# A list-scheduling planner is given TensorE's switch costs, the wait of a dependent operation, a fixed engine for early products, and other seeds

## The chip, the core and the metric

The kernel runs on one core of a Trainium2 chip. The metric is the time of one execution on the device in microseconds. The profiled execution is one such run with the hardware profiler on; its span goes from the first to the last recorded instruction and is a little shorter than its own time.

## The reference

Attention with a decaying state (per batch, head and step), then a feed-forward block with a spatial mixing over the 768 steps. Sizes: 4 batches, 8 heads, 768 steps, 48 dimensions per head (384 in all), 1024 hidden units.

```python
for t in range(S):
    cur = np.einsum('bhd,bhe->bhde', u[None] * kt, vt)
    y[:, :, t] = np.einsum('bhd,bhde->bhe', rt, state + cur)
    state = w[None, :, :, None] * state + np.einsum('bhd,bhe->bhde', kt, vt)
...
h = np.maximum(x @ w_in, 0.0)
u, v = (h[..., :d_ff // 2], h[..., d_ff // 2:])
v_n = (v - mu) / np.sqrt(var + 1e-06)
v_s = np.einsum('ts,bsd->btd', w_spatial, v_n) + b_spatial[None, :, None]
return ((u * v_s) @ w_out).astype(np.float32)
```

x is the attention's y with the heads side by side; mu and var are taken over v's 512 columns.

## The kernel before

The attention is worked in 24 chunks of 128 steps (6 for each batch). For chunk m, `load_chunk` brings the tiles rk, rs, ks and rkv; `prep` scales rk by the decays (L569 on GpSimd or L571 on VectorE for the first 13 chunks, one VectorE operation at L575 for the others), makes three products of rs and ks and one of diag with dg, reduces rs to dg (L580), and from chunk 8 on copies parts of rk into the tile A. TensorE then has three short steps for the chunk, called the mixer's: `scores` (s, 32 matmuls of 64x64, L611), `products` (r, 32 or 16 matmuls of 64x48, L630), both into one PSUM tile ps, and `apply` (y, 64 to 96 matmuls of 128x32 by 64 columns, L692) into xp. Between them `state` masks the scores (L659), carries the state from chunk to chunk (L673, L677, L679) and copies blocks for y. `fin` splits y into a high part (L332) and a low part (L729) of x.

The feed-forward tiles are made of matmuls of 128x128 by 384 or 512 columns in three terms, high by high, high by low and low by high (L735, L736, L737): `moe_v` and `moe_u` (x by w_in), `moe_sp` (spatial mixing, in a form with seven products), `moe_out` (by w_out). Between them stand the normalization of v, splits into high and low parts (`split_v`), and the gate. In the beginning VectorE, ScalarE and TensorE turn the weights, which come as 64-bit numbers, into high and low parts (`from_f64`, L457 to L480).

None of the order is written by hand. Every step is a task in `Plan`: it has one or more ways (engine and estimated cost), the tasks before it, the buffers that it takes, and a due time. `dues` works the due times out backwards from a nominal order of TensorE's tiles. `shake` then shifts the due times and the engines' leanings at random, once for each number in `SEEDS`. `run` plays the tasks through in time: it takes for each engine the best of the ready tasks, by a key that puts those that can start at once (within 0.02 us) first, by due time, and those that can start only later behind; the task's instructions are emitted in that order. A task with several ways gets the engine on which it would end first, with a `lean` added to discourage one. `BEHIND` and `SIGNAL` are the times from an operation's end to another engine's start; before the change a task on the same engine as its predecessor could start at the predecessor's end:

```python
can = max([clear] + [b.free if b.engine == e else b.end + SIGNAL[e] for b in t.before])
late = at <= free.get(e, 1.0) + 0.02
key = (0, t.due, t.place) if late else (1, at, t.due, t.place)
```

`Clock` and `Fetch` model TensorE's clock and its instruction fetch. All loads and most stores are issued by SP's queue in the planner's order (L344, L375).

Of the kernel before, what the change touches and what calls it, by code (L numbers as in the profile page):

```python
# [19 lines left out]
P = 128  # L20
# [20 lines left out]
AHEAD = 0.3  # L41
ALONE = 1000.0
CALM, LATE = 80.0, dict(DVE=1.0, SP=1.0)
SEEDS = (654236, 40537, 227094, 802348, 927760, 243010, 847265, 669742, 767280, 592966, 398425, 483486, 769239,
         558881, 534905, 557774, 619884, 911825, 37087, 256776, 431103, 948404, 736101, 744100, 112095, 746069,
         318923, 577348, 283095, 953310, 564408, 778876, 669839, 55107, 864631, 805599, 160787, 198409, 373592,)
BIAS = dict(DVE=3.0, ACT=3.5)
MOST_IN, MOST_OUT = 2, 1


BEHIND = dict(PE=0.2, DVE=0.08, ACT=0.094, POOL=0.055, SP=0.0)
SIGNAL = dict(PE=0.05, DVE=0.03, ACT=0.03, POOL=0.08, SP=0.03)
# [10 lines left out]
class Task:  # L63
    def __init__(self, ways, lag, nominal):
        self.ways, self.lag, self.nominal = [Way(*w) for w in ways], lag, nominal
        self.cost = min(w.cost for w in self.ways)
        self.engine = None
# [45 lines left out]
class Plan:  # L113
# [92 lines left out]
    def run(self):  # L206
# [4 lines left out]
        count = {k: len(u) for k, u in self.users.items()}  # L211
        last = dict.fromkeys(self.users, 0.0)
        free, line, landed, clock, fetch, bank = {}, 0.0, [], Clock(), Fetch(), {}
        self.port = 0.0
        while ready:
            best, ahead = {}, dict(free)
            for t in sorted(ready, key=lambda t: (t.due, t.place)):
                takes = [k for k in t.bufs if k not in self.slot]
                if any(len(self.slots[k[0]]) <= self.spare(k, count) for k in takes):
                    continue  # L220
                if any(k[0] in self.FIFO and self.turn[k] != self.given.get(k[0], 0) for k in takes):
                    continue
                clear = max([1.0] + [min(self.slots[k[0]])[0] for k in takes])
                found = None
                for way in t.ways:
                    e = way.engine
                    can = max([clear] + [b.free if b.engine == e else b.end + SIGNAL[e] for b in t.before])
                    if t.bank:
                        can = max([can] + [x + SIGNAL[e] for o, x in bank.items() if o != e])
                    at = max(can, ahead.get(e, 1.0)) if len(t.ways) > 1 else max(can, free.get(e, 1.0))  # L230
                    if way.nbytes:
                        at = max(self.lane(at, landed), t.due - self.AHEAD_IN)
                    end = (self.landing(line, at, way.nbytes) if way.nbytes else at + self.shared_cost(way, at)) + (way.lean if t.due < CALM or way.lean > 99.0 else LATE.get(e, 0.0))
                    if found is None or end < found[0]:
                        found = (end, e, can, way)
                _, e, can, way = found
                at = max(can, free.get(e, 1.0))
                if way.nbytes:
                    at = max(self.lane(at, landed), t.due - self.AHEAD_IN)
                if can <= ahead.get(e, 1.0) + AHEAD and not way.nbytes:  # L240
                    ahead[e] = max(can, ahead.get(e, 1.0)) + way.cost
                late = at <= free.get(e, 1.0) + 0.02
                key = (0, t.due, t.place) if late else (1, at, t.due, t.place)
                if e not in best or key < best[e][0]:
                    best[e] = (key, at, t, way)
            if not best:
# [39 lines left out]
def fused_kernel(ctx, tc, rkT, rkvE, rkvL, wT, uB, w_in, w_sp, b_sp, w_out, out):  # L286
    nc = tc.nc
    E = mybir.EngineType
    for e in (E.PE, E.DVE, E.Activation, E.Pool, E.SP):
        ctx.enter_context(tc.manual_schedule(engines={e}))  # L290
    EARLY, STATS, EC = 13, 1, FIRST_CHUNKS
    CLASSIC = (0,)
    SUM_IN, SUM_OUT = range(NK), []
    LOAD_IN = {0: -50.0, 1: -50.0}
# [15 lines left out]
    def pe(cost, f, r, w, count, nominal=None, holds=()):  # L310
        behind = 0.11 if count > 15 and count % 9 and count % 4 == 0 else 0.2
        plan.add([("PE", cost, f, False, 0, 0.0, behind)], r, w, nominal=nominal, holds=holds).count = count
# [248 lines left out]
    def prep(m):  # L561
# [12 lines left out]
        else:  # L574
            dve(1024, lambda: nc.vector.tensor_tensor(out=rk(), in0=rk(), in1=tt.unsqueeze(1).to_broadcast(  # L575
                [P, 2, NP, C]), op=ALU.mult), [RK, *TT], [r_, k_], cost=1.14, two=True)
        n_, k0 = (lambda: T[RS]), (lambda: T[KS])
        pair(DM, lambda: dict(out=n_(), in0=n_(), in1=k0(), op=ALU.mult), [RS, KS], [rn], lean=LEAN)
        pair(DM, lambda: dict(out=n_(), in0=n_(), in1=ub, op=ALU.mult), [rn, ("c", "ub")], [rn], lean=LEAN)
        dve(DM - 8, lambda: nc.vector.tensor_reduce(out=tile_of(DG, [P, H]), in_=n_().rearrange("s (h d) -> s h d", h=H),  # L580
                                                axis=AX.X, op=ALU.add), [rn], [DG])
        pair(DM, lambda: dict(out=k0(), in0=k0(), in1=tn_f, op=ALU.mult), [KS, rn, *TN], [kn], lean=LEAN)
        pair(432, lambda: dict(
            out=a().rearrange("s b q z t -> s (b q z) t"), in0=diag.unsqueeze(1).to_broadcast([P, H, HC]),
            in1=T[DG].unsqueeze(2).to_broadcast([P, H, HC]), op=ALU.mult), [DG, ("c", "diag")], [A], lean=LEAN)
# [18 lines left out]
    def scores(m):  # L604
        PS, RK = ("ps", m), ("rk", m)

        def f():
            ps, rk = pst, T[RK]
            for p2, z, s0, t0, j, b in QUAD:
                hd, hf, p, o = slice(64 * j, 64 * j + 64), j ^ b, 2 * b + p2, (2 * p2 + z) * HC  # L610
                nc.tensor.matmul(ps[64 * hf:64 * hf + 64, b, o:o + HC], rk[hd, 1, p, s0:s0 + 64],  # L611
                                 rk[hd, 0, p, t0:t0 + 64], start=True, stop=True, skip_group_check=True)

        pe(0.51, f, [RK + ("r",), RK + ("k",)], [PS + ("s",)], 32, nominal=(2 * m, 1))

    def products(m):
        PS, KS, RV = ("ps", m), ("ks", m), ("rkv", m)
# [16 lines left out]
        pe(0.47 if m % NC < NC - 1 else 0.25, f, [KS + ("kn",), RV, ("c", "pz")], [PS + ("k",)], 32 if m % NC < NC - 1 else 16, nominal=(2 * m, 2))  # L634
# [49 lines left out]
    def apply(m):  # L684
# [29 lines left out]

        if m < EC:
            pe(1.48 if c else 1.14, f, [SB + (1,), *([SB + (0,)] if c else []), ("a", m), ("rk", m, "r"), RV], [XP],
               96 if c else 72, nominal=(2 * m + 2, 0))
            return
        pe(1.03, f, [RV, RV + ("s1",), *([RV + ("s0",)] if c else []), *(("A", m, ("a", h, 0)) for h in range(2)),
                    *(("A", m, ("r", t, 2 * b)) for b in range(2) for t in range(2))], [XP], 64, nominal=(2 * m + 2, 0))  # L720

    def fin(m):
        b, c = divmod(m, NC)
# [21 lines left out]
    def moe_v(b, c, nominal):  # L745
# [15 lines left out]
        if (b, c) == (0, 0):  # L761
            for low in range(2):
                for j in range(NK):
                    pe(0.46 - 0.23 * low, lambda j=j, low=low: by_part(j, low),
                       xkeys(b, [c])[0:2 - low] + [("wi", 1, j, "hl"[low])], [PM], 2 - low, nominal=(*nominal, low, j),
                       holds=[VB])
        else:
            pe(2.1, f, xkeys(b, [c]) + wkeys(*(("wi", 1, j) for j in range(NK))), [PM], 9, nominal=nominal, holds=[VB])
        i = c % 3
        q = lambda: tile_of(Q, [P, 48])  # L770
        vs = lambda: tile_of(VB, [P, 3, DH])[:, i]
# [81 lines left out]
    def moe_u(b, t, d, nominal):  # L853
# [30 lines left out]
    def moe_sp(b, d, q, nominal, final=False):  # L884
# [6 lines left out]
        def product(PM, first, holds=(), terms=((q, q),)):  # L891
            def f():
                pm = tile_of(PM, [P, 512])[:, 0:TH]
                for n, (k, w) in enumerate(terms):
                    t = T["t", (b, d, k)]
                    for i in range(NT):
# [66 lines left out]
    def moe_out(b, t, i, nominal, blocks=(range(ND),)):  # L963
# [3 lines left out]
        for n, ds in enumerate(blocks):  # L967
# [6 lines left out]
            pe(0.5235 * len(ds), f, wkeys(*(gt_key(b, t, d) for d in ds), *(("wo", d) for d in ds)) + ([PM] if n else []), [PM], 3 * len(ds), nominal=nominal[n])  # L974
# [155 lines left out]
```

## Time and profile before

| | |
|---|---|
| time, median of 3 runs | 333.07 us (332.94 to 335.96) |
| the profiled execution's own time | 333.48 us |
| its span | 331.8 us, 10954 instructions |
| TensorE busy | 314.4 us, 95% of the span, 4574 matmuls |
| VectorE, GpSimd, ScalarE busy | 247.3, 243.6, 199.3 us |
| HBM read, written | 43.58 MB, 4.72 MB |

Engines are PE (TensorE matmul), PEld (its weight loads, beside the matmuls), DVE (VectorE), ACT (ScalarE), POOL (GpSimd), SP (SyncE, which issues DMAs). The ends of matmuls are modelled, so their starts say more than their durations. A helper's line (L327 for a product that may run on VectorE or GpSimd, L332 for a copy) stands for many steps; the tile's name tells them apart.

### The profile page before, as it was taken

The numbers are of one execution on the slowest core, as the hardware profiler recorded it, in microseconds if no ns is written. First come the engines' busy times: TensorE is split into PE (matmuls) and PEld (weight loads), VectorE is DVE, ScalarE is ACT, GpSimd is POOL, SyncE is SP. The second block draws the span as 40 slices with busy tenths as digits, with TensorE's granted clock in tenths as the row PEclk, the third lists the DMA queues.
The fourth block names the chain that finished last, engine by engine and source line by source line (L and its number), as shares of the span: only waits on it lengthen the run. The fifth ranks groups of instructions, "written<-read, shape, count | busy, mean of one in ns | idle before, by whom it ended". The sixth has DMA issues, their size and how long they took to land.

```text
span 331.8 us, 10954 instructions
## 1 busy us (share of the span) xinstructions
PE 314.4 (95%) x4574; PEld 282.5 (85%) x4574; DVE 247.3 (75%) x466; ACT 199.3 (60%) x488; POOL 243.6 (73%) x228
## 2 busy tenths in 40 slices
PE   2967999999999999999999999999999999999995
PEld 1445788899999798889879988999988999999995
DVE  6999988989991878988999477987899642305940
ACT  4346856565653878793676378887679534524322
POOL 3868989878999989999989254888988323628700
PEclk9999899999999999999999999999999999999999
DMA  6999568577274744241453345453531001020012
GB/s 205 413 409 385 174 232 289 173 256 250 61 242 153 270 157 138 86 152 52 150 157 103 131 129 189 147 188 126 175 97 28 3 24 49 0 73 0 1 49 95
DMA packets 22033, 49.86 MB, mean 150 GB/s; under 512 B 2656, under 2 KB 12832, under 8 KB 21984
## 3 DMA queue, kind: packets, MB, share of 16 engines
q1 hardware_dynamic: 21840, 49.07, 43.6%
q8 instruction: 36, 0.59, 0.7%
q14 instruction: 13, 0.11, 0.1%
q10 hardware_dynamic: 144, 0.10, 0.1%
HBM read 43.58 MB, written 4.72 MB: 146 GB/s over the span
## 4 chain that ended last, share of the span: by engine, by line
PE 71%; POOL 9%; DMA 9%; DVE 7%; issue 2%; SPq 1%; ACT 1%; POOLq 0%; ACTq 0%
PE pm L735 21%; PE pm L737 19%; PE pm L736 19%; PE xp L692 6%; DMA rk<-rkT 4%; PE ps L611 3%; DMA wa<-w_in 3%; PE ps L630 2%; POOL rs L327 2%; DMA rs<-rkvE 2%; POOL t L327 2%; POOL X L327 1%; POOL a L327 1%; POOL ks L327 1%; POOL wb L327 1%
## 5 line engine op out<-in xcount | busy, mean ns | idle before, releaser
L735 PE MATMUL pm<-wa,t 128*128 128x384 f32 x120 | 41.8, 348 | 0.1
L737 PE MATMUL pm<-wa,t 128*128 128x384 f32 x120 | 40.5, 337 | 0.3 <-DVE t L327 0.3
L736 PE MATMUL pm<-wa,t 128*128 128x384 f32 x120 | 40.3, 336 | 0.0
L327 POOL TENSOR_TENSOR rs<-rs,ks 128x384 f32<-128x384 f32 x22 | 25.9, 1180 | 11.8 <-DMA ks<-rkvL 7.3
L327 POOL TENSOR_TENSOR t<-vs,t 128x384 fp32r<-128x384 f32 x24 | 28.3, 1185 | 8.4 <-ACT t L332 8.1
L735 PE MATMUL pm<-x,wi_h 128*128 128x384 f32 x93 | 32.6, 351 | 0.0
L737 PE MATMUL pm<-x,wi_l 128*128 128x384 f32 x93 | 31.2, 336 | 0.0
L736 PE MATMUL pm<-x,wi_h 128*128 128x384 f32 x93 | 31.2, 335 | 0.0
L906 DVE TENSOR_TENSOR g<-pm,bb 128x384 f32<-128x384 f32 x32 | 17.4, 550 | 17.2 <-PE pm L737 17.0
L735 PE MATMUL pm<-wi_h,x 128*128 128x512 f32 x69 | 28.2, 408 | 0.5 <-ACT x L332 0.5
L735 PE MATMUL pm<-wo_h,gt 128*128 128x384 f32 x84 | 28.6, 340 | 0.0
L737 PE MATMUL pm<-wi_h,x 128*128 128x512 f32 x69 | 27.9, 405 | 0.4 <-DVE x L729 0.4
L737 PE MATMUL pm<-wo_h,gt 128*128 128x384 f32 x84 | 28.3, 336 | 0.0
L736 PE MATMUL pm<-wo_l,gt 128*128 128x384 f32 x84 | 28.2, 336 | 0.0
L327 POOL TENSOR_TENSOR a<-diag,dg 128x512 f32<-128x512 f32 x20 | 23.7, 1187 | 5.8 <-DVE dg L580 3.4
L736 PE MATMUL pm<-wi_l,x 128*128 128x512 f32 x69 | 27.6, 400 | 0.0
L327 POOL TENSOR_TENSOR gt<-u,gt 128x384 fp32r<-128x384 f32 x16 | 18.0, 1133 | 13.0 <-ACT gt L332 13.0
L597 ACT COPY A<-rk 64x256 f32<-64x256 f32 x50 | 20.2, 404 | 7.4 <-DVE rk L571 4.1
L735 PEld LDWEIGHTS pm<-wa,t 128*128 128x128 f32 x120 | 22.5, 188 | 1.4 <-DVE g L906 0.4
L332 ACT CAST gt<-u 128x384 fp32r<-128x384 f32 x28 | 14.0, 513 | 15.4 <-DVE u L327 8.8
L327 POOL TENSOR_TENSOR t<-X,t 128x384 fp32r<-128x384 f32 x17 | 21.9, 1287 | 1.8 <-ACT t L332 1.8
L737 PEld LDWEIGHTS pm<-wa,t 128*128 128x128 f32 x120 | 22.6, 188 | 0.6 <-DVE t L327 0.6
(180 smaller groups left out, 958.3 us busy)
## 6 DMA issues: line engine op xcount, KB each, us to landing
rk<-rkT SPq DMA_DIRECT2D x24, 512.0 KB, 4.6
rkv<-rkvL SPq DMA_DIRECT2D x16, 512.0 KB, 4.0
out<-ob SPq DMA_DIRECT2D x23, 192.0 KB, 1.9
wa<-w_in SPq DMA_DIRECT2D x6, 512.0 KB, 8.0
rkv<-rkvE SPq DMA_DIRECT2D x8, 384.0 KB, 6.1
rs<-rkvL SPq DMA_DIRECT2D x16, 192.0 KB, 2.4
ks<-rkvL SPq DMA_DIRECT2D x16, 192.0 KB, 4.2
wb<-w_sp SPq DMA_DIRECT2D x6, 384.0 KB, 7.3
```

The source lines that it names most:

```text
L327: plan.add([(e, cost[e], lambda e=e: engine[e].tensor_tensor(**f()), True, 0, lean if e == "DVE" else 0.0) for e in ways.split()], r, w)
L332: emit = dict(DVE=lambda: nc.vector.tensor_copy(**f()), ACT=lambda: nc.scalar.copy(f()["out"], f()["in_"]))
L597: ("ACT", (n + 250) / 1200, lambda out=out, p=p, h=h: nc.scalar.copy(out(), source(p, h))),
L611: nc.tensor.matmul(ps[64 * hf:64 * hf + 64, b, o:o + HC], rk[hd, 1, p, s0:s0 + 64], rk[hd, 0, p, t0:t0 + 64], start=True, stop=True, skip_ ...
L630: nc.tensor.matmul(ps[64 * j:64 * j + D, b, o:o + D], kn[hs, kc:kc + D], ve[hs, h, z, p, slice(0, D) if m < EC else slice(16 * h, 16 * h + ...
L692: nc.tensor.matmul(xp[32 * p:32 * p + 32, o:o + HC], lhsT, rhs, start=p not in began, stop=True, skip_group_check=True, tile_position=(0, ...
L735: nc.tensor.matmul(o, lh, rh, start=first, stop=False, skip_group_check=free)
L736: nc.tensor.matmul(o, lh, rl, start=False, stop=False, skip_group_check=free)
L737: nc.tensor.matmul(o, ll, rh, start=False, stop=last, skip_group_check=free)
L906: dve(TH, lambda: nc.vector.tensor_tensor(out=g(K), in0=T[PM][:, 0:TH], in1=other(), op=ALU.add), [PM, ("c", "bb"), *r], [K])
```

## The change

The planner gets three numbers more and one rule:

- `SWITCH`: a TensorE step that follows one of another kind costs more, by the pair of kinds. Kinds are s, r, y for the mixer's steps and b for everything else.
- `STAY`: among TensorE's steps, one of the same class (b, or the mixer's three together) as the step before it is ranked as though it were due 1 us earlier.
- `CHAIN`: an operation whose predecessor ran on the same engine can start 0.115 us (VectorE) or 0.11 us (ScalarE) after that one's end.
- `QUIET`: in chunks 0 to 5, the four choosable products of `prep` lean away from VectorE by 1000 instead of 4, that is, they go to GpSimd.

A few costs are changed in the last digit, and all 39 seeds are others. No task is added or removed.

```diff
-SEEDS = (654236, 40537, 227094, 802348, 927760, 243010, 847265, 669742, 767280, 592966, 398425, 483486, 769239,
...
+SEEDS = (903816, 933540, 289621, 240081, 214286, 400392, 384699, 187708, 469736, 101467, 893305, 384172, 738380,
...
+CHAIN = dict(PE=0.0, DVE=0.115, ACT=0.11, POOL=0.0, SP=0.0)
+SWITCH = {"bs": 0.095, "br": 0.095, "by": 0.095, "sb": 0.215, "sy": 0.11, "rb": 0.105, "yb": 0.105}
+STAY = 1.0
...
-        self.port = 0.0
+        self.port, self.kind = 0.0, "b"
...
-                    can = max([clear] + [b.free if b.engine == e else b.end + SIGNAL[e] for b in t.before])
+                    can = max([clear] + [b.free + CHAIN[e] if b.engine == e else b.end + SIGNAL[e] for b in t.before])
...
-                key = (0, t.due, t.place) if late else (1, at, t.due, t.place)
+                due = t.due - STAY if e == "PE" and (t.kind == "b") == (self.kind == "b") else t.due
+                key = (0, due, t.place) if late else (1, at, due, t.place)
...
             if e == "PE":
+                cost += SWITCH.get(self.kind + t.kind, 0.0)
+                self.kind = t.kind
...
+    QUIET = 6
...
-        pair(DM, lambda: dict(out=n_(), in0=n_(), in1=k0(), op=ALU.mult), [RS, KS], [rn], lean=LEAN)
-        pair(DM, lambda: dict(out=n_(), in0=n_(), in1=ub, op=ALU.mult), [rn, ("c", "ub")], [rn], lean=LEAN)
+        lean = ALONE if m < QUIET else LEAN
+        pair(DM, lambda: dict(out=n_(), in0=n_(), in1=k0(), op=ALU.mult), [RS, KS], [rn], lean=lean)
+        pair(DM, lambda: dict(out=n_(), in0=n_(), in1=ub, op=ALU.mult), [rn, ("c", "ub")], [rn], lean=lean)
...
-        pe(0.51, f, [RK + ("r",), RK + ("k",)], [PS + ("s",)], 32, nominal=(2 * m, 1))
+        pe(0.51, f, [RK + ("r",), RK + ("k",)], [PS + ("s",)], 32, nominal=(2 * m, 1), kind="s")
...
-            pe(2.1, f, xkeys(b, [c]) + wkeys(*(("wi", 1, j) for j in range(NK))), [PM], 9, nominal=nominal, holds=[VB])
+            pe(2.09, f, xkeys(b, [c]) + wkeys(*(("wi", 1, j) for j in range(NK))), [PM], 9, nominal=nominal, holds=[VB])
...
-            pe(1.57, f, xs + wkeys(*(("wi", 0, j) for j in range(NK))), [PM], 9, nominal=nominal, holds=[U])
+            pe(1.56, f, xs + wkeys(*(("wi", 0, j) for j in range(NK))), [PM], 9, nominal=nominal, holds=[U])
```

## Rows read from the trace of the kernel before

**Rows 1.** The page, busy time, share of the span and instructions of each engine.

```profile
PE 314.4 (95%) x4574; PEld 282.5 (85%) x4574; DVE 247.3 (75%) x466; ACT 199.3 (60%) x488; POOL 243.6 (73%) x228
```

**Rows 2.** Busy time by stretch (columns in the first row).

```profile
core 0: us, PE busy (x) PEld busy (x) DVE busy (x) ACT busy (x) POOL busy (x), PEclk, DMA share, GB/s
0.00:31.50 31.50, 19.29 (x415) 12.25 (x415) 26.90 (x50) 14.04 (x31) 21.07 (x33) 1.00 0.94 356
20.00:31.50 11.50, 6.93 (x171) 4.48 (x171) 11.26 (x21) 5.16 (x13) 7.67 (x8) 1.00 1.04 408
31.50:35.00 3.50, 3.49 (x19) 2.37 (x23) 3.40 (x8) 2.76 (x8) 3.42 (x5) 0.51 0.43 169
35.00:328.00 293.00, 291.36 (x4152) 267.93 (x4144) 216.69 (x409) 181.90 (x449) 219.10 (x192) 1.00 0.39 129
```

**Rows 3.** TensorE's waits: waiter, waited-for, us in total, times, longest us.

```profile
PE pm L427 <- POOL A L416: 4.0, 1, 4.0
...
PE xp L692 <- ACT A L644: 1.9, 1, 1.9
PE ps L611 <- POOL rk L569: 1.3, 2, 1.0
```

**Rows 4.** Timeline of TensorE around mixer steps: start, us, line, tiles, shape, count.

```profile
57.11 0.34 PE L737 MATMUL pm<-x,wi_l 128*128 128x384 f32 x1
57.38 0.69 PE L611 MATMUL ps<-rk 64*64 64x64 f32 x32
57.89 0.59 PE L630 MATMUL ps<-rkv,ks 64*48 64x48 f32 x32
58.41 0.44 PE L735 MATMUL pm<-x,wi_h 128*128 128x384 f32 x1
58.70 0.34 PE L736 MATMUL pm<-x,wi_h 128*128 128x384 f32 x1
58.87 0.34 PE L737 MATMUL pm<-x,wi_l 128*128 128x384 f32 x1
...
71.15 0.69 PE L611 MATMUL ps<-rk 64*64 64x64 f32 x32 [0.33 <-POOL rk L569]
71.78 0.44 PE L735 MATMUL pm<-wa,t 128*128 128x384 f32 x1
...
85.46 1.10 PE L692 MATMUL xp<-A,rkv 128*32 128x64 f32 x64
86.49 0.44 PE L735 MATMUL pm<-wa,t 128*128 128x384 f32 x1
86.77 0.34 PE L736 MATMUL pm<-wa,t 128*128 128x384 f32 x1
...
108.70 1.10 PE L692 MATMUL xp<-A,rkv 128*32 128x64 f32 x64
109.73 0.69 PE L611 MATMUL ps<-rk 64*64 64x64 f32 x32
```

**Rows 5.** The same timeline, first row of the first and of the last visit.

```profile
11.88 1.13 PE L611 MATMUL ps<-rk 64*64 64x64 f32 x32
...
274.68 1.10 PE L692 MATMUL xp<-A,rkv 128*32 128x64 f32 x64
```

**Rows 6.** Timeline of VectorE, an independent and a dependent successor.

```profile
9.48 0.68 DVE L571 TENSOR_TENSOR rk<-rk,pm 128x512 f32<-128x512 f32 x1
10.07 0.68 DVE L459 SCALAR_TENSOR_TENSOR wa<-wa,pm 128x512 uint32<-128x512 uint32 x1
10.79 0.69 DVE L461 TENSOR_SCALAR pm<-wa 128x512 uint32<-128x512 uint32 x1
```

**Rows 7.** The chain that ended last, 19 to 32 us: start, us, what.

```profile
19.16 0.70 DVE pm L457
...
30.99 0.48 DVE x L729
```

**Rows 8.** Timelines of VectorE and GpSimd near 48 us.

```profile
47.18 0.55 DVE L327 TENSOR_TENSOR ks<-ks,tn 128x384 f32<-128x384 f32 x1
48.42 1.01 POOL L327 TENSOR_TENSOR rs<-rs,ks 128x384 f32<-128x384 f32 x1 [1.29 <-DMA ks<-rkvE]
```

**Rows 9.** Waits of SP's DMA queue, columns as in Rows 3.

```profile
SPq L344 <- PE xp L692: 35.5, 15, 5.6
```

More of the change, by code (lines that the diff above doesn't have):

```diff
@@ L43 @@
 CALM, LATE = 80.0, dict(DVE=1.0, SP=1.0)
-SEEDS = (654236, 40537, 227094, 802348, 927760, 243010, 847265, 669742, 767280, 592966, 398425, 483486, 769239,
-         558881, 534905, 557774, 619884, 911825, 37087, 256776, 431103, 948404, 736101, 744100, 112095, 746069,
-         318923, 577348, 283095, 953310, 564408, 778876, 669839, 55107, 864631, 805599, 160787, 198409, 373592,)
+SEEDS = (903816, 933540, 289621, 240081, 214286, 400392, 384699, 187708, 469736, 101467, 893305, 384172, 738380,
+         350979, 812521, 758905, 432271, 775034, 238406, 297387, 104577, 907208, 191139, 764255, 495759, 338786,
+         886938, 253099, 555284, 297324, 391479, 270977, 946005, 628996, 426649, 259701, 875528, 861998, 110189,)
 BIAS = dict(DVE=3.0, ACT=3.5)
@@ L66, in __init__ @@
         self.cost = min(w.cost for w in self.ways)
-        self.engine = None
+        self.engine, self.kind = None, "b"
         self.count, self.bank = 0, False
@@ L308, in tile_of, with pe @@
         return T[key]
-    def pe(cost, f, r, w, count, nominal=None, holds=()):
+    def pe(cost, f, r, w, count, nominal=None, holds=(), kind="b"):
         behind = 0.11 if count > 15 and count % 9 and count % 4 == 0 else 0.2
-        plan.add([("PE", cost, f, False, 0, 0.0, behind)], r, w, nominal=nominal, holds=holds).count = count
+        t = plan.add([("PE", cost, f, False, 0, 0.0, behind)], r, w, nominal=nominal, holds=holds)
+        t.count, t.kind = count, kind
     def dve(n, f, r, w, cost=None, two=False, due=None):
@@ L577, in prep @@
         n_, k0 = (lambda: T[RS]), (lambda: T[KS])
-        pair(DM, lambda: dict(out=n_(), in0=n_(), in1=k0(), op=ALU.mult), [RS, KS], [rn], lean=LEAN)
-        pair(DM, lambda: dict(out=n_(), in0=n_(), in1=ub, op=ALU.mult), [rn, ("c", "ub")], [rn], lean=LEAN)
+        lean = ALONE if m < QUIET else LEAN
+        pair(DM, lambda: dict(out=n_(), in0=n_(), in1=k0(), op=ALU.mult), [RS, KS], [rn], lean=lean)
+        pair(DM, lambda: dict(out=n_(), in0=n_(), in1=ub, op=ALU.mult), [rn, ("c", "ub")], [rn], lean=lean)
         dve(DM - 8, lambda: nc.vector.tensor_reduce(out=tile_of(DG, [P, H]), in_=n_().rearrange("s (h d) -> s h d", h=H),
                                                 axis=AX.X, op=ALU.add), [rn], [DG])
-        pair(DM, lambda: dict(out=k0(), in0=k0(), in1=tn_f, op=ALU.mult), [KS, rn, *TN], [kn], lean=LEAN)
+        pair(DM, lambda: dict(out=k0(), in0=k0(), in1=tn_f, op=ALU.mult), [KS, rn, *TN], [kn], lean=lean)
         pair(432, lambda: dict(
             out=a().rearrange("s b q z t -> s (b q z) t"), in0=diag.unsqueeze(1).to_broadcast([P, H, HC]),
-            in1=T[DG].unsqueeze(2).to_broadcast([P, H, HC]), op=ALU.mult), [DG, ("c", "diag")], [A], lean=LEAN)
+            in1=T[DG].unsqueeze(2).to_broadcast([P, H, HC]), op=ALU.mult), [DG, ("c", "diag")], [A], lean=lean)
         if m >= EC:
@@ L632, in f @@
                                  start=True, stop=True, skip_group_check=True)
-        pe(0.47 if m % NC < NC - 1 else 0.25, f, [KS + ("kn",), RV, ("c", "pz")], [PS + ("k",)], 32 if m % NC < NC - 1 else 16, nominal=(2 * m, 2))
+        pe(0.47 if m % NC < NC - 1 else 0.27, f, [KS + ("kn",), RV, ("c", "pz")], [PS + ("k",)], 32 if m % NC < NC - 1 else 16, nominal=(2 * m, 2), kind="r")
     def sblk(n):
@@ L716, in apply @@
             pe(1.48 if c else 1.14, f, [SB + (1,), *([SB + (0,)] if c else []), ("a", m), ("rk", m, "r"), RV], [XP],
-               96 if c else 72, nominal=(2 * m + 2, 0))
+               96 if c else 72, nominal=(2 * m + 2, 0), kind="y")
             return
         pe(1.03, f, [RV, RV + ("s1",), *([RV + ("s0",)] if c else []), *(("A", m, ("a", h, 0)) for h in range(2)),
-                    *(("A", m, ("r", t, 2 * b)) for b in range(2) for t in range(2))], [XP], 64, nominal=(2 * m + 2, 0))
+                    *(("A", m, ("r", t, 2 * b)) for b in range(2) for t in range(2))], [XP], 64, nominal=(2 * m + 2, 0), kind="y")
     def fin(m):
@@ L899, in f @@
                             n == len(terms) - 1 and i == NT - 1, True)
-            pe(1.57 * len(terms), f, wkeys(*(("t", (b, d, k)) for k, w in terms),
+            pe(1.56 * len(terms), f, wkeys(*(("t", (b, d, k)) for k, w in terms),
                                           *(("ws", w, i) for k, w in terms for i in range(NT))), [PM],
@@ L972, in f @@
                     mm3(pm[:, 0:DM], gt[:, 0, o], gt[:, 1, o], wo_h[:, d, :], wo_l[:, d, :], d == ds_all[0], d == ds_all[-1])
-            pe(0.5235 * len(ds), f, wkeys(*(gt_key(b, t, d) for d in ds), *(("wo", d) for d in ds)) + ([PM] if n else []), [PM], 3 * len(ds), nominal=nominal[n])
+            pe(0.52 * len(ds), f, wkeys(*(gt_key(b, t, d) for d in ds), *(("wo", d) for d in ds)) + ([PM] if n else []), [PM], 3 * len(ds), nominal=nominal[n])
         if (b, t, i) == (B - 1, 1, 2):
```

## The prediction

> **What bounds the kernel now.** I read the page's busy times first: TensorE (PE) is busy 314.4 of 331.8 us, the next engine 247.3 [rows 1]. The busy times by stretch say where the other 17.4 us lie [rows 2]: 12.2 in the first 31.5 us, 1.6 in the 293 us between 35 and 328, the rest behind the last matmul. Between 31.5 and 35 us TensorE is busy but its granted clock is 0.51, that is 1.2 instead of 2.4 GHz: 3.5 x 0.49 = 1.7 us of lost work. The list of waits names what TensorE stood for, the long ones all in the beginning [rows 3]. So from 35 us on only less work on TensorE itself shortens the kernel, and before that only an earlier first result of other engines.
>
> Of TensorE's own work the timeline shows a part that computes nothing [rows 4]. Call the moe and spatial tiles b, the mixer's scores s, its state products r, its application y. One b tile's matmuls of 384 columns start 0.17 us apart (58.70 to 58.87). The last of them before s takes 0.27 (57.11 to 57.38), so entering the mixer costs 0.10. The first one behind r takes 0.29 (58.41 to 58.70) and behind y 0.28 (86.49 to 86.77), so leaving costs 0.11. Leaving from s costs 0.12 more: s takes 0.63 when b follows (71.15 to 71.78) and 0.51 when r follows (57.38 to 57.89). I call a stretch of mixer steps with b on both sides a visit. The trace has 45 visits, the first at 11.88, the last at 274.68 us [rows 5]: 10 end in s (0.33 each), 22 in r and 13 in y (0.21 each), 10 x 0.33 + 35 x 0.21 = 10.7 us.
>
> **The change, part by part.** No instruction is added or dropped; which engine runs some of them and their order is decided anew.
>
> *SWITCH and STAY.* The planner now charges these switches, and a step of the kind that TensorE is at counts as due 1 us earlier. Only steps that are ready compete, so a visit merges with the next where one b tile or less stands between them and both were nearly due. The timeline has eleven such gaps of 1.8 us or less. Two lie between two s steps, which can't join, as both write the same PSUM tile and VectorE must empty it in between; two lead from r to y, and y needs VectorE's and ScalarE's work on s and r first. That leaves seven. I take seven visits fewer at the mean 10.7 / 45 = 0.24 us: **-1.6 us**. Bounds: no merge, 0; every y(m) with s and r of m+1, 25 visits of 0.21 left, 10.7 - 5.3 = -5.4. I am near the lower bound since many steps stand 2 to 15 us apart, more than 1 us of due can join. A mixer step that waits for company delays what hangs on it; behind it SP's queue waits for y to free the load buffers, 35.5 us in 15 waits [rows 9], so its loads move by as much, and TensorE's 1.6 us of idle time over 293 us says that this slack exists.
>
> The Trainium skill (TensorEngine Tiling (Array Packing), Key Properties) says that a change of tiling mode drains the array; y runs as 128x32, s and r as 64x64. By that rule joining y to s pays one drain inside the visit. The trace doesn't bear it out: y takes 1.03 us whether s follows (108.70 to 109.73) or b (85.46 to 86.49) [rows 4]. By the rule this term would be 7 x 0.11 = 0.8 instead of 1.6 us.
>
> *CHAIN.* A VectorE operation that reads what the one before it wrote now counts as startable 0.115 us later. The timeline agrees in size [rows 6]: L571 to an independent L459 is 0.59 us from start to start, L459 to the L461 that depends on it 0.72, both on 512 elements: 0.13. The planner now puts any ready operation between such two. It matters where VectorE sets the end: the chain that ended last runs through VectorE without a break from 19.16 to 31.46 us [rows 7], and eight of its pieces follow their own producer. 8 x 0.13 = 1.0 at most; I take half, as there isn't always a wanted operation to fill in: **-0.5 us**, bounds 0 and -1.0, on the loss side see the last rival. ScalarE gets the same 0.11, and is idle for 17.5 of the first 31.5 us [rows 2]; there I take nothing, bounds 0 and -0.1.
>
> *QUIET.* In chunks 0 to 5 the four choosable products of prep (24 in all) go to GpSimd. In the trace 23 of them are there already; the one on VectorE is ks<-ks,tn at 47.18 us, 0.55 us. On GpSimd one takes about 1.0. GpSimd stands idle for 1.29 us before 48.42, for a load [rows 8], so it fits there: 0. Without that cover GpSimd runs 1.0 us later, and TensorE's wait for GpSimd's rk at L569 (1.3 us in two waits [rows 3]) could grow by it: bounds 0 and +1.0.
>
> *Retuned costs* (2.1 to 2.09, 1.57 to 1.56 and the like) change no operation. By themselves 0.
>
> *New seeds.* All 39 random shifts of due times and leanings are others, so every engine's order changes in places. After 35 us only 1.6 us of idle time are left to win, and stalls could come in; the nearest rows for a stall are TensorE's own longest waits in the loaded stretch, 1.9 and 1.0 us [rows 3]. I take 0, bounds -1.6 and +2.9 (both of them once more).
>
> Sum: against the profiled execution's 333.48 us, -1.6 - 0.5 = 331.4. That execution is 0.41 above the median of 333.07, so on the median's scale **331.0 us**.
>
> **Rivals.** *The beginning is reordered for the better.* From 20 to 31.5 us TensorE is busy 6.93 of 11.5 us, 4.57 idle, and the stretch at half clock behind it costs 1.7 [rows 2]: 6.3 us can be won if other seeds bring the chunks' low parts and GpSimd's rk sooner. For it: only there is idle time. Against it: the DMA share is 1.04 in this stretch [rows 2], so loads can't come much sooner, and VectorE has hardly a gap. Half of it, with the visits: 333.07 - 1.6 - 3.15 = 328.3; range 326.5 to 329.7.
>
> *Nothing joins.* Readiness, not the due time, sets the visits: s at 71.15 came straight behind a wait for GpSimd [rows 4], and the next chunk's rk must have been landed and scaled. Then the count stays near 45 and only the CHAIN term is left: 332.6; range 331.8 to 334.5, the upper end with the stalls of new seeds.
>
> *Joining pays only half.* As the skill's rule has it, as a mechanism: the time between y and s is hidden in y's own 1.03 us, and y alone is charged for a later one. Then 333.07 - 0.8 - 0.5 = 331.8. Against it stand the rows above.
>
> *Slower.* CHAIN ranks an operation that waits 0.115 us below any that is ready, however far its due time. In the VectorE chain of 19 to 31.5 us, each of the eight dependent pieces can thus get an unneeded one of 0.6 us ahead of it, 0.6 - 0.13 = 0.47 each: 8 x 0.47 = 3.8 us later weights wi_l and low parts, and TensorE, longer idle, once more 1.7 us at half clock. 333.07 + 5.5 - 1.6 = 337.0. It decides (over 336.4) from seven of the eight pieces with the clock. For it: the key puts late operations first without a limit. Against it: most of what is ready on VectorE there is a conversion or a state step that TensorE needs as well.
>
> **How the numbers follow.** Forecast 0.40 (its own range 329.2 to 332.0), the better beginning 0.25, nothing joins 0.20, half pay 0.05, slower 0.10. 1% of 333.07 is 3.3 us, about what a measurement of this kernel can tell from no change: faster is under 329.7, slower over 336.4. Faster: 0.25 and an eighth of the forecast's chance, 0.30. Slower: 0.10. Same: 0.60. The range of 8 in 10 goes from 327.8 (some 0.08 of the better beginning below it) to 334.5 (the slower case and a little of the third above it).
>
> **What the profile after would show.** Visits: about 38 in TensorE's timeline where 45 were, and TensorE's busy time some 1.6 us shorter with the same 4574 matmuls. CHAIN: VectorE's pieces between 19 and 31 us start 0.60 apart where 0.72 stood. QUIET: ks<-ks,tn of chunk 5 on GpSimd, VectorE's count of it down by one. Seeds: TensorE's idle time between 35 and 328 us near 1.6. I am wrong if the count of visits stays over 43 or falls under 32, if the first 31.5 us hold another idle time than 10 to 13 us, if the stretch at half clock is gone or doubled, or if waits of over 3 us in all appear after 35 us.

## The result and the profile after

The changed kernel takes **337.2 us** (median of 20 runs, 335.12 to 341.3) beside 333.56 us for the kernel before (20 runs, 331.97 to 335.96) on the same chip: a ratio of 1.0096, with an interval of 1.0072 to 1.0119. It is slower by about 1%, 3.2 us. (The medians are 3.6 us apart; the ratio is not their quotient and leaves out the one slow run of 341.3 us.) The profiled execution of after takes 336.15 us, 1.05 less than the median, with a span of 334.4, 2.6 us more than the span before.

Lines have moved by 8 or 9: what was L611, L630, L692 and L735 to L737 is L620, L639, L701 and L744 to L746. The page of after, busy times, and then busy time by stretch, to be laid beside [rows 1] and [rows 2], which has the columns:

```profile
PE 310.3 (93%) x4574; PEld 283.3 (85%) x4574; DVE 241.0 (72%) x462; ACT 193.2 (58%) x477; POOL 250.4 (75%) x237
```

```profile
0.00:31.50 31.50, 16.28 (x375) 11.22 (x379) 25.60 (x48) 13.43 (x30) 21.44 (x33) 0.93 0.94 359
20.00:31.50 11.50, 5.47 (x135) 3.98 (x139) 8.95 (x17) 5.17 (x12) 8.07 (x8) 0.82 1.01 400
31.50:35.00 3.50, 3.50 (x55) 2.81 (x46) 2.56 (x6) 2.65 (x8) 2.95 (x3) 0.61 0.45 136
35.00:328.00 293.00, 287.79 (x4144) 266.84 (x4143) 212.45 (x408) 176.28 (x438) 226.04 (x202) 1.00 0.39 129
```

TensorE works 4.1 us less (314.4 to 310.3) and stands 6.7 us more. The timeline has 26 visits where 45 were, and 4 of them end in s, 18 in r, 4 in y. At the prices of [rows 4] that is 4 x 0.33 + 22 x 0.21 = 5.9 us instead of 10.7, so 4.8 saved; the busy time fell by 4.1, most of that. The idle time went from 12.2 to 15.2 us before 31.5 us (+3.0), from 1.6 to 5.2 between 35 and 328 us (+3.6), and by 0.1 behind the last matmul. -4.1 + 3.0 + 3.6 + 0.1 = 2.6, the difference of the spans.

TensorE's waits in after (waiter, waited-for, us in total, times, longest), for [rows 3]:

```profile
PE xp L701 <- issue: 4.1, 1, 4.1
PE pm L435 <- POOL A L424: 4.0, 1, 4.0
...
PE pm L744 <- DVE g L915: 2.5, 3, 1.5
PE ps L639 <- POOL ks L335: 2.3, 2, 1.9
PE pm L746 <- POOL t L335: 0.9, 1, 0.9
PE pm L746 <- DVE x L738: 0.8, 1, 0.8
```

Two new kinds of wait are there. One is a single stand of 4.1 us that no operation of another engine ends ("issue"). The others are short waits for VectorE's and GpSimd's results (g, t, x, rk) far behind the start: they make most of the 5.2 us behind 35 us, where 1.6 stood.

The stand, in TensorE's timeline of after (start, us, line, tiles, shape, count, idle before it):

```profile
22.74 0.40 PE L767 MATMUL pm<-wi_l,x 128*128 128x512 f32 x1
25.07 0.57 PE L639 MATMUL ps<-rkv,ks 64*48 64x48 f32 x32 [1.93 <-POOL ks L335]
25.57 0.88 PE L701 MATMUL xp<-rk,A 128*32 128x64 f32 x48
26.27 0.41 PE L701 MATMUL xp<-a,rkv 128*32 128x64 f32 x16
30.78 1.08 PE L701 MATMUL xp<-a,rkv 128*32 128x64 f32 x32 [4.10 <-issue]
...
39.44 0.45 PE L874 MATMUL pm<-x,wi_h 128*128 128x384 f32 x1
```

It cuts one y step in two, after 16 of 48 matmuls. Counted from the start it comes behind matmul 347; a shorter stand of 0.61 us comes at 19.47 us, behind matmul 220. Busy time of after up to each of the two, whose PE counts show this:

```profile
0.00:30.50 30.50, 15.56 (x347) 10.50 (x347) 25.60 (x48) 13.43 (x30) 21.44 (x33) 0.95 0.95 362
0.00:19.40 19.40, 10.29 (x220) 6.77 (x220) 16.05 (x31) 8.26 (x18) 13.33 (x25) 1.00 0.89 334
```

The two places are 127 matmuls apart (single records can be missing from a trace). The page lists an instruction queue, q8, in both kernels: 36 packets, 0.59 MB, that is 16.4 KB for each 4574 / 36 = 127 matmuls of TensorE. I take this as blocks of instructions, one for every 128 matmuls, that come through the DMA engines, and a stand "for issue" at a block's edge as a wait for the block. The queues that moved data in three windows, first after from 18.2 to 28.3 us, then after from 28.3 to 29.5, then before from 23.1 to 24.3 (queue, packets, MB, share of 16 engines):

```profile
q1 hardware_dynamic: 1662, 4.16, 103.5%
...
q1 hardware_dynamic: 240, 0.45, 98.1%
q8 instruction: 1, 0.02, 5.0%
...
q1 hardware_dynamic: 150, 0.49, 101.1%
q8 instruction: 1, 0.02, 5.4%
```

With edges every 128 matmuls back from 347 (219, 91), the packet for the block behind 347 was on its way from 28.40 us in after and from 23.19 in before, 5.2 us earlier. What differs is the work around matmul 251, some 30 behind the preceding edge. TensorE stood 1.93 us near it in both kernels, but not at the same place. Before's timeline there:

```profile
22.69 0.54 PE L692 MATMUL xp<-rk,A 128*32 128x64 f32 x24
25.17 0.90 PE L692 MATMUL xp<-rk,A 128*32 128x64 f32 x24 [1.93 <-ACT A L644]
26.17 0.88 PE L692 MATMUL xp<-a,rkv 128*32 128x64 f32 x48
...
37.30 0.50 PE L735 MATMUL pm<-wi_h,x 128*128 128x512 f32 x1
```

Before, TensorE passed matmul 251 at 22.69 us and the wait for ScalarE came 24 matmuls behind it: the packet went out as that wait began, and when the 96 short matmuls up to the edge were used up, the block was there. In after the wait (for GpSimd's ks) comes right behind matmul 251; the 96 short matmuls behind the wait were used up in 1.6 us (25.07 to 26.68), and the packet set out only at 28.40, 3.3 us after 25.07. That the block is requested when TensorE passes about matmul 251 is inferred from these times, and the mark is a rough one. From passing it to the packet it is 0.5 us in before, 0.7 to 1.6 in seven kernels of the experiments, and 3.3 to 3.5 in after and four others (e2, e3, e6, e8); in e11 the packet sets out 0.4 us ahead of it. What makes the difference no run parts: the loads fill the DMA engines in both, q1 with 106.7% in before's 0.5 us and 103.9% in after's 3.3. Behind the same number of matmuls (582), after is at 39.44 us where before is at 37.30: 2.1 of the 2.6 us between the spans are lost by then.

The Trainium skill (Runtime: NRT & Kernel Launch, Instruction fetch mechanics) says that an engine's instructions are refilled in blocks of 16 KiB while the current ones run, and that crossing a block's edge is mostly hidden. The block's size agrees with q8's 16.4 KB a packet; "hidden" doesn't hold here: one crossing cost 4.10 us.

### The profile page after: what moved, and what is told of

Read it like the earlier page. It is cut to its first block, busy times and chain, and to the rows that moved or that the text cites. A ratio compares the mean times of both kernels' runs of the same rounds, so it can differ in the third digit from the quotient of the medians.

```text
span 334.4 us, 10976 instructions
## 1 busy us (share of the span) xinstructions
PE 310.3 (93%) x4574; PEld 283.3 (85%) x4574; DVE 241.0 (72%) x462; ACT 193.2 (58%) x477; POOL 250.4 (75%) x237
## 4 chain that ended last, share of the span: by engine, by line
PE 60%; DMA 12%; POOL 12%; DVE 7%; issue 4%; SPq 3%; ACT 2%; POOLq 0%; DVEq 0%; ACTq 0%
PE pm L744 17%; PE pm L746 16%; PE pm L745 16%; DMA rk<-rkT 6%; PE xp L701 6%; DMA ks<-rkvE 4%; POOL t L335 3%; PE ps L620 3%; POOL X L335 2%; POOL rs L335 2%; SPq L352 2%; DMA ks<-rkvL 1%; POOL wb L335 1%; PE ps L639 1%; POOL ks L335 1%
## 5 line engine op out<-in xcount | busy, mean ns | idle before, releaser
L744 PE MATMUL pm<-wa,t 128*128 128x384 f32 x120 | 41.1, 343 | 1.5 <-DVE g L915 1.5
L746 PE MATMUL pm<-wa,t 128*128 128x384 f32 x120 | 40.5, 337 | 0.0
L335 POOL TENSOR_TENSOR t<-vs,t 128x384 fp32r<-128x384 f32 x27 | 33.5, 1255 | 3.3 <-ACT t L340 3.1
L335 POOL TENSOR_TENSOR rs<-rs,ks 128x384 f32<-128x384 f32 x19 | 22.0, 1155 | 17.2 <-DMA ks<-rkvL 9.1
L744 PE MATMUL pm<-x,wi_h 128*128 128x384 f32 x93 | 31.9, 343 | 0.0
L746 PE MATMUL pm<-x,wi_l 128*128 128x384 f32 x93 | 31.2, 336 | 0.0
L745 PE MATMUL pm<-x,wi_h 128*128 128x384 f32 x93 | 31.2, 335 | 0.0
L335 POOL TENSOR_TENSOR a<-diag,dg 128x512 f32<-128x512 f32 x19 | 20.2, 1062 | 14.4 <-ACT A L606 10.2
L744 PE MATMUL pm<-wo_h,gt 128*128 128x384 f32 x84 | 28.7, 341 | 0.0
L744 PE MATMUL pm<-wi_h,x 128*128 128x512 f32 x69 | 27.9, 405 | 0.6 <-DVE rk L579 0.4
L746 PE MATMUL pm<-wo_h,gt 128*128 128x384 f32 x84 | 28.2, 336 | 0.0
L746 PE MATMUL pm<-wi_h,x 128*128 128x512 f32 x69 | 27.2, 395 | 0.8 <-DVE x L738 0.8
L335 POOL TENSOR_TENSOR gt<-u,gt 128x384 fp32r<-128x384 f32 x21 | 22.5, 1082 | 4.2 <-ACT gt L340 4.2
L335 POOL TENSOR_TENSOR X<-vs,X 128x384 f32<-128x384 f32 x10 | 12.2, 1224 | 17.4 <-ACT vs L826 17.0
L744 PEld LDWEIGHTS pm<-wa,t 128*128 128x128 f32 x120 | 22.5, 188 | 2.7 <-ACT t L340 1.8
L335 POOL TENSOR_TENSOR ks<-ks,tn 128x384 f32<-128x384 f32 x22 | 24.1, 1097 | 0.0
L335 POOL TENSOR_TENSOR u<-g,u 128x384 f32<-128x384 f32 x20 | 22.2, 1120 | 1.5 <-DVE pm L809 1.2
```

What stands on the lines that cost most here:

```text
L335: plan.add([(e, cost[e], lambda e=e: engine[e].tensor_tensor(**f()), True, 0, lean if e == "DVE" else 0.0) for e in ways.split()], r, w)
L744: nc.tensor.matmul(o, lh, rh, start=first, stop=False, skip_group_check=free)
L745: nc.tensor.matmul(o, lh, rl, start=False, stop=False, skip_group_check=free)
L746: nc.tensor.matmul(o, ll, rh, start=False, stop=last, skip_group_check=free)
```

## The experiments

The planner plays everything through in one go, so one changed number moves every operation behind it. To hold the rest of the order fixed, e1 to e9 don't plan: they take a list of all operations with their engines, in the order in which one of the two planners emitted them, and only a part of the list is exchanged. A diff on such a list is shown as what it stands for. (Which buffer of its kind a tile gets is fixed in the list too. e8 has exactly after's buffers; in e3 and e6 62 of the 621 are others, in e4 and e7 77 are others than in before.) All ratios are to the kernel before, run beside each; "idle" is TensorE's between 35 and 328 us in the profile, and the last column but one is its longest wait for issue (a dash: none in the list of waits).

| kernel | visits | idle, us | longest "issue" wait, us | ratio (interval) |
|---|---|---|---|---|
| before | 45 | 1.6 | - | 1 |
| after | 26 | 5.2 | 4.1 | 1.0096 (1.0072 to 1.0119) |
| e1_old_start | 28 | 4.9 | 0.6 | 0.9991 (0.9956 to 1.0026) |
| e2_new_start | 43 | 4.4 | 3.3 | 1.0155 (1.0103 to 1.0208) |
| e6_new_start_old_loads | 26 | 6.4 | 4.2 | 1.0208 (1.0175 to 1.0240) |
| e7_old_start_new_loads | 45 | 3.0 | 0.4 | 1.0018 (0.9995 to 1.0041) |
| e8_sixteen_more | 26 | 6.7 | 1.3 | 1.0048 (1.0019 to 1.0078) |
| e3_split | 40 | 8.3 | 4.4 | 1.0278 (1.0216 to 1.0339) |
| e4_merge | 34 | 4.8 | 0.8 | 1.0023 (0.9990 to 1.0056) |
| e5_old_start_sums | 28 | 5.0 | 0.9 | 0.9960 (0.9927 to 0.9994) |
| e9_six_moves | 28 | 4.4 | 0.8 | 0.9964 (0.9943 to 0.9985) |
| e10_old_seeds | 40 | 9.8 | 0.7 | 1.0436 (1.0399 to 1.0474) |
| e11_new_seeds | 37 | 7.5 | 0.3 | 1.0293 (1.0244 to 1.0342) |
| e12_no_stay | 36 | 6.2 | 1.7 | 1.0117 (1.0066 to 1.0167) |

### Start and rest exchanged

```diff
-order = changed planner's list
+order = [what before's planner starts in its first 35 us] + [the others in the changed planner's order]   # e1
-order = list of the planner before
+order = [what the changed planner starts in its first 35 us] + [the others in the order before]           # e2
```

> The steps that the planner before had planned for its first 35 us, in its order, and behind them the rest in the changed planner's order. Theory 'the start': the changed kernel loses in its first 40 us (matmul 582 starts at 39.44 us, before at 37.30: +2.1 in the profiles, and up to +3.5 where another stretch at half clock is added), and the rest is +0.3 or less. Then this kernel comes out within 0.5 us of the kernel before, 333.1 to 334.1 with a median of 333.56. Theory 'the rest': other engines' results come too late behind 35 us since the mixer's steps are joined, and the start is only noise; then it stays near the changed kernel's 337, at 336 or more. TensorE's visits to the mixer: 28 (45 before, 26 changed).

> The mirror image: the changed planner's steps of its first 35 us, then the rest in the order of the planner before. Theory 'the start': 335.7 to 337, with TensorE standing some 4 us in the middle of an apply near 27 us for nothing that another engine owes it. Theory 'the rest': 333 to 334. 43 visits.

e1 takes 333.92 us beside 333.75, as theory 'the start' had it: the changed order loses nothing behind the old start, so the loss lies in the start. It wins nothing either. Its waits behind 35 us and its busy time there:

```profile
PE pm L744 <- DVE g L915: 2.8, 3, 1.2
PE pm L746 <- POOL t L335: 0.7, 1, 0.7
...
35.00:328.00 293.00, 288.12 (x4108) 267.63 (x4096) 209.44 (x405) 176.20 (x436) 224.99 (x201) 1.00 0.40 130
```

TensorE is busy 311.2 us, 3.2 less than before, and idle for 293 - 288.12 = 4.9 us where 1.6 stood, 3.3 more: the joined visits' gain is paid back in waits. In e2 a stand of 3.29 us is there again, at matmul 347, though all behind 35 us is old. Its 339.86 us is over the forecast (335.7 to 337). Its profile shows two things that weren't forecast: a granted 0.50 from 25.9 to 36.0 and from 43.0 to 46.2 us, and 4.4 us of idle time behind 35 us where before had 1.6.

```profile
30.97 1.08 PE L692 MATMUL xp<-a,rkv 128*32 128x64 f32 x32 [3.29 <-issue]
```

### What delays the instruction block

```diff
-loads = SP's first 33 loads in the changed planner's order
+loads = SP's first 33 loads in the order before              # e6, all else as after
-loads = SP's first 33 loads in the order before
+loads = SP's first 33 loads in the changed planner's order   # e7, all else as before
...
-for z, p2, hf in ((z, p2, hf) for z in range(2) for p2 in range(2) for hf in range(2)):
+for z, p2, hf in [(z, p2, hf) for z in range(2) for p2 in range(2) for hf in range(2)] * (2 - b):   # e8, at L431
```

e8 issues eight small products of the first microseconds a second time, with the same result: 16 more matmul records early, so that every later block edge lies 16 matmuls earlier in the same work.

> The changed kernel with SyncE's first 33 loads in the order of the kernel before, all else as it was. In the changed kernel the third block of TensorE's instructions comes at 28.4 us (23.2 before), and TensorE stands 4.1 us for it. Theory 'loads': the block waits behind the four w_sp loads issued from 14.47 us on; then with the old loads it comes near 23 us, the stand is gone, and the time is 333.5 to 334.5. Theory 'request': the block is asked for only when TensorE gets some 30 matmuls past the edge of the block before, and TensorE stood at that place for GpSimd; then it comes at 28 us still and the time stays 336 to 338.

> The mirror image: the kernel before with SyncE's first 33 loads in the changed kernel's order. Theory 'loads': the third block of instructions comes at 28 us, TensorE stands 3 to 4 us for it, 336.5 to 338. Theory 'request': the block comes near 23 us and the time stays within 1 us of 333.6, but for what other loads coming in another order cost.

> The changed kernel with eight small matmuls of its first step written twice (16 records more, in time in which TensorE is idle anyway), so that every later matmul stands 16 places further on in the instruction blocks. Theory 'request': the third block is now asked for 16 matmuls earlier in the work, that is before TensorE's wait for GpSimd's ks at 25 us in place of behind it; it comes 3 to 5 us earlier than 28.4, the 4.1 us stand shrinks to under 1, and the time falls by 2 to 4 us, to 333.5 to 335. Theory 'loads': the block comes at 28 us as before, and the time stays at 337.

The order of the loads is not it: e6 has the old one and stands 4.17 us at the same matmul, with its packet at 29.55 us; e7 has the new one and no stand there, with its packet at 24.15 us, and takes 334.26 us, as forecast by 'request'. (e6 takes 340.94 us, more than either theory said: with the old loads its new start also waits 5.0 us for the weights wi_l where after waited 3.2, and the granted clock is 0.50 from 29.9 to 40.1 us.) What matters is which work stands around the edge: in e8, with the new start and the new loads, the packet goes out at 23.12 us and the y step runs through. e8's timeline:

```profile
25.25 0.57 PE L639 MATMUL ps<-rkv,ks 64*48 64x48 f32 x32 [0.58 <-POOL ks L335]
25.75 0.88 PE L701 MATMUL xp<-rk,A 128*32 128x64 f32 x48
26.44 0.85 PE L701 MATMUL xp<-a,rkv 128*32 128x64 f32 x48
29.39 0.95 PE L620 MATMUL ps<-rk 64*64 64x64 f32 x32 [2.10 <-POOL rk L577]
...
37.50 0.61 PE L874 MATMUL pm<-x,wi_h 128*128 128x384 f32 x2
...
58.01 0.30 PE L639 MATMUL ps<-rkv,ks 64*48 64x48 f32 x7 [1.27 <-issue]
```

The stand is gone, and the start's loss with it: the work that after reaches at 39.44 us e8 reaches at 37.50, before at 37.30, though TensorE now waits 2.10 us for GpSimd's rk, which the stand had covered. Yet e8 takes 336.02 us, between the two forecasts: the ratio falls from 1.0096 to 1.0048, 1.6 of the 3.2 us, and the two intervals still overlap a little. In its profile, whose span of 334.4 us is that of after, the lead is lost again behind the start. The moved edges bring a stand of 1.27 us at 58.01 us, where after ran through. And at 238 us, where both kernels wait for the same sum g of VectorE, they go on at the same time, though e8 came 0.5 us earlier; after first, then e8:

```profile
238.28 0.41 PE L744 MATMUL pm<-wa,t 128*128 128x384 f32 x1 [1.49 <-DVE g L915]
238.29 0.41 PE L744 MATMUL pm<-wa,t 128*128 128x384 f32 x1 [1.99 <-DVE g L915]
```

So in these profiles the stand makes the start's loss, and without it TensorE waits elsewhere for what it had gained. The clock plays a part in the start as well. e8 has two stretches of 3.4 us at half clock that are full of work (from 19.4 and from 29.7 us); in after, of two such stretches, the first lay in the stand and cost nothing:

```profile
27.40:30.80 3.40, 0.02 (x4) 0.02 (x4) 2.08 (x5) 0.09 (x1) 2.71 (x3) 0.50 1.06 408
30.80:34.20 3.40, 3.40 (x67) 2.92 (x68) 1.76 (x4) 1.87 (x6) 2.15 (x3) 0.50 0.51 158
```

So after lost 3.4 x 0.5 = 1.7 us to the clock, as before did [rows 2], and e8 twice that.

### Visits alone

```diff
-TensorE: ... y(m) s(m+1) b ...
+TensorE: ... y(m) b s(m+1) ...            # e3: after, 14 joined visits broken where the next b was ready
-TensorE: ... mixer step, b, b, mixer step ...
+TensorE: ... both mixer steps, b, b ...   # e4: before, 13 mixer steps moved ahead, no other engine touched
```

> The changed kernel's order, with one feed-forward tile put between the apply and the scores or products behind it at 14 places after 35 us: 40 visits in place of 26, nothing else moved. If a visit costs 0.21 us wherever it stands and TensorE sets the end throughout: 14 x 0.21 = +2.9 us over the changed kernel (about 340), and TensorE's idle time behind 35 us stays at 5.2 us. If the other engines set the end behind 35 us (the joined order leaves them no slack): idle time falls by as much as the switches add, and the time rises by less than 1 us.

> The kernel before with TensorE's order alone edited: 13 of the mixer's steps after 35 us are moved ahead to join the visit before them, where their inputs are there by then; 34 visits in place of 45. If the price of a visit is all there is: 18 + 7 at 0.21 and 9 at 0.33 are 8.2 us where 10.7 stood, -2.4 us, 331.1. If joining costs as much in waits as it saves: no change, 333 to 334, with TensorE's idle time behind 35 us up from 1.6 to about 4 us.

Neither goes by the price of a visit alone, and neither theory on e3 holds. e3 should have cost 14 x 0.21 = 2.9 us; it costs 1.82% of 333.6, 6.1 us, over after. In its profile, the slowest of its four executions, TensorE is busy 317.3 instead of 310.3 us, and idle behind 35 us for 8.3 instead of 5.2. Its waits for g are 6.6 us in all instead of 2.5. Of them, the two longest and what the clock did behind each:

```profile
PE pm L744 <- DVE g L915: 6.6, 6, 2.0
...
243.06 0.42 PE L744 MATMUL pm<-wa,t 128*128 128x384 f32 x1 [1.99 <-DVE g L915]
...
266.19 0.44 PE L744 MATMUL pm<-wb,t 128*128 128x384 f32 x1 [1.75 <-DVE g L915]
...
243.70:246.90 3.20, 3.20 (x12) 3.20 (x11) 3.20 (x3) 1.62 (x5) 3.20 (x3) 0.50 0.00 0
267.60:270.80 3.20, 3.20 (x12) 3.13 (x10) 2.34 (x11) 0.88 (x3) 1.34 (x3) 0.50 0.02 5
```

Each of these two waits is followed within 1.5 us by a stretch at half clock that is all work: 1.6 us more for each. So the 2.9 us are paid, and waits and clock come on top. It doesn't follow from the length of the wait alone: behind e8's wait of 1.99 us, shown above, TensorE worked on at the full clock.

```profile
238.30:241.70 3.40, 3.40 (x23) 3.15 (x27) 3.40 (x5) 2.11 (x6) 3.40 (x3) 1.00 0.00 0
```

e4, with 9 visits that end in s and 25 in r or y, should have cost 9 x 0.33 + 25 x 0.21 = 8.2 instead of 10.7 us, 2.5 less, and saved nothing (335.05 beside 333.75 us), near the second theory: its idle time went from 1.6 to 4.8 us, in new short waits. Behind two of them, which end at 140.41 and 141.88 us, the clock is at half as well, which takes another 3.4 x 0.5 = 1.7 us; before had no such stretch behind 35 us.

```profile
PE ps L611 <- DVE a L659: 1.6, 2, 0.9
PE ps L630 <- POOL wb L327: 1.0, 1, 1.0
...
142.00:145.40 3.40, 3.40 (x98) 3.11 (x96) 0.53 (x2) 1.51 (x4) 3.40 (x4) 0.50 0.24 63
```

### The waits behind 35 us

The sums g (L915) for which e1's TensorE waits stand on VectorE behind operations that are needed later.

```diff
-VectorE: ... dg(L589) ... g(L915) ...
+VectorE: ... g(L915) ... dg(L589) ...   # e5: e1 with four VectorE operations moved ahead, at three places
+                                        # e9: e5 with two more, at two further places
```

> The order of e1 (the start of the kernel before, the rest of the changed one) with four sums of VectorE (g<-pm at L915) moved ahead of one to three other VectorE operations, at the three places where TensorE waited for them, 0.74 + 1.23 + 0.87 = 2.8 us. If those waits are what holds the joined order back: -2.5 us against e1's 333.9, 331.4, faster than both kernels. If VectorE as a whole is late there, the waits reappear at the operations that were passed: 333 to 334.

> The order of e5 with two more VectorE operations moved ahead, at places where TensorE waited in its profile: a low part of x (0.88 us, L738) ahead of a copy of rk and a masking, and a sum (1.42 us, L915) ahead of a copy of a. If single late operations are the cause, 1.5 us less than e5's 332.5: 331.0. If VectorE lags as a whole, no change from e5: 332.5.

e5 takes 332.49 us beside 333.68, e9 332.48 beside 333.52: both are 0.4% faster than before, not as fast as forecast (331.4 and 331.0), and the step from e1 to e5 lies within their intervals. The waits moved more than they went; of e5, behind 35 us:

```profile
PE pm L744 <- DVE g L915: 1.4, 1, 1.4
PE pm L744 <- DVE rk L579: 1.0, 1, 1.0
...
```

Idle time is 5.0 us, as in e1 (4.9), so the profile doesn't show where the 0.4% come from; and two more moves win nothing. So it isn't only a few operations at a wrong place: where TensorE has less to do, it seems to catch up with engines that deliver at their old pace, as at e8's and after's sum g at 238 us. Why they are no faster (VectorE is busy 211 of 293 us in e5) no run separates.

### Planner and seeds

```diff
-SEEDS = (903816, 933540, 289621, ...
+SEEDS = (654236, 40537, 227094, ...     # e10: after with the seeds of before
...
-SEEDS = (654236, 40537, 227094, ...
+SEEDS = (903816, 933540, 289621, ...    # e11: before with the seeds of after
...
-STAY = 1.0
+STAY = 0.0                              # e12: after
```

> The changed planner whole (SWITCH, STAY, CHAIN, QUIET) with the 39 seeds of the kernel before; 40 visits. Theory 'the seeds carry the plan' (they were searched for one planner and are 39 arbitrary numbers for another): well slower than both kernels, over 340. Theory 'the rules carry it': 333 to 338.

> The planner before with the 39 new seeds; 37 visits. Theory 'the seeds carry the plan': over 340. Theory 'the rules carry it': within 2 us of the kernel before, 332 to 336.

> The changed kernel with STAY at 0, SWITCH, CHAIN, QUIET and the new seeds kept; 36 visits where it has 26. By the price of a visit alone, 10 x 0.24 = 2.4 us over the changed kernel, 339.6. If every edit of the planner throws the seeds out of step: 342 or more, with waits over 8 us behind 35 us.

Each half alone is far worse than both together: +4.4% and +2.9% against +1.0%, with 9.8 and 7.5 us of idle time behind 35 us. That bears out theory 'the seeds carry the plan' for these two exchanges. It doesn't hold for every edit of the planner: e12, with STAY at 0 and the new seeds, takes 337.2 us like after, which meets neither of its forecasts (339.6, and 342 or more). It has ten visits more than after: once more the count of visits doesn't tell the time. It also shows the block's edge in a third order, with the packet at 23.7 us:

```profile
23.75 0.87 PE L701 MATMUL xp<-a,rkv 128*32 128x64 f32 x46
26.35 0.27 PE L701 MATMUL xp<-a,rkv 128*32 128x64 f32 x2 [1.73 <-issue]
```

The packet takes about 1.0 us (6.3% of 16 engines in a window of 1 us), and TensorE goes on 1.6 us after that; in after it is 28.40 + 0.96 to 30.78, 1.4 us. Over all kernels here, in the stands of over 0.3 us at the edges behind 219 and 347 and at 58 us in e8, TensorE goes on 2.2 to 2.8 us after the packet sets out, whatever held it up before.

## Why the prediction was wrong

It said 331.0 us, 327.8 to 334.5, with 0.10 for slower. The kernel takes 337.2. Two terms of the sum failed: the visits' -1.6, which TensorE saved and the time didn't, and the 0 for a new order, which came out as a stand in the start that the forecast had no row for. Step by step:

- **Visits: right price, wrong count, wrong worth.** Busy time fell by 4.1 us, as 19 visits fewer at [rows 4]'s prices give 4.8. I forecast seven fewer because I went through the old order for gaps that 1 us of due could close. With another plan the old order says little on this: 36 to 40 visits come out of the same steps in e10 to e12. The worse fault is that I carried the term into the time. "TensorE's 1.6 us of idle time over 293 us says that this slack exists" was the wrong reading: it says that TensorE was hardly kept waiting at its old pace, not that the others could keep up with a faster one. e1 gives the whole gain back (-3.2 busy, +3.3 idle); on the kernel before, e4 gives its 2.5 us back in waits (+3.2) and to the clock (+1.7).
- **CHAIN: the spacing came in part, the gain didn't.** VectorE's timeline of after, in the stretch that the forecast named:

```profile
19.76 0.68 DVE L469 TENSOR_SCALAR pm<-wa 128x512 uint32<-128x512 uint32 x1
20.48 0.69 DVE L484 SCALAR_TENSOR_TENSOR pm<-wa,pm 128x512 f32<-128x512 uint32 x1
21.21 0.70 DVE L486 TENSOR_TENSOR pm<-pm,wa 128x512 f32<-128x512 f32 x1
...
26.15 0.70 DVE L465 TENSOR_SCALAR pm<-wa 128x512 uint32<-128x512 uint32 x1
26.75 0.69 DVE L469 TENSOR_SCALAR pm<-wa 128x512 uint32<-128x512 uint32 x1
```

  Two dependent pairs still start 0.72 and 0.73 apart as in [rows 6]; later ones, with other work between producer and reader, 0.60. But VectorE no longer set the start's end: from 20 to 31.5 us it is busy 8.95 us instead of 11.26 [rows 2], and the chain that ended last goes through GpSimd's ks (to 25.02 us) and the stand (26.68 to 30.78) instead.
- **QUIET at 0** holds as far as the trace shows: VectorE has no product into ks in the first 75 us any more, and TensorE's new waits for ks come from chunks whose products were on GpSimd before too.
- **New seeds at 0, bounds -1.6 to +2.9: this is the step that failed most.** The new order cost 2.1 us in the start in the profile and, by e1, the whole difference to before. I bounded a stall by TensorE's longest waits for other engines. The wait for its own instructions wasn't among them; yet q8 stood on the page, and [rows 4]'s mixer steps, 32 matmuls in half a microsecond, use up a block of 128 in about 2 us. The term's name is too narrow: the stand behind matmul 347 is in neither e10 (new rules, old seeds) nor e11 (old rules, new seeds), so it belongs to the order that rules and seeds make together.
- **The rival "slower" had the number (337.0) and not the mechanism**, which is luck. It let CHAIN hold up the VectorE chain of 19 to 31.5 us, plus a second stretch at half clock. That chain no longer set the path, and the second stretch cost after nothing. The signs that I had named for being wrong all came: 26 visits (under 32), 15.2 us idle in the start (over 13), 5.2 us behind 35 (over 3), and the stretch at half clock doubled.
- **"Joining pays only half"** falls: y takes 1.03 us with s behind it in after too (121.47 to 122.50), and the busy time fell by about what the full price gives.

What stays open: why a block's packet sets out 0.5 us behind the inferred mark in one kernel and 3.3 in another, and how far the other executions of e8 lose their lead at the places where the profiled one does.

## What to carry to other kernels

A saving on the busiest engine counts only as far as its feeders run ahead of it; look how early their results come, not how seldom the engine waits. A list of random seeds goes with the cost model that it stands beside: exchanging either alone cost 2.9 and 4.4% here, though setting STAY to 0 cost nothing. Whoever changes the model gets a new order, and has to measure that order, not the edit. And where a burst of short matmuls follows a wait, look where TensorE's instruction blocks end: 16 matmul records more ahead of the edge took away a stand of 4.1 us here, and brought one of 1.27 us at another edge.

## What the runs showed of the hardware

TensorE's instructions came in blocks of 128 matmuls, 16.4 KB each, on their own DMA queue beside the loads, and in the stands TensorE went on 2.2 to 2.8 us after the block's packet set out. With the changed planner's start a stand fell behind matmul 347 in four kernels (4.10, 3.29, 4.38 and 4.17 us), and a shorter one of 1.73 us in e12; with the old start or the edge moved by 16 records it was gone there. Behind 35 us, waits of 1.99 and 1.75 us in e3 were followed by a stretch at a granted 0.50 that cost 1.6 us each; one of 1.99 us in e8 was not.
